# Gram products of the weights after their sign step, in a rebuilt order: sparse attention, a Fourier mixing step and a two-layer network on one core

## The chip, the cores and the metric

The kernel runs on one core of a Trainium2 chip. A core has a matrix engine (TensorE, PE; the profile keeps its weight loads apart as PEld), a vector engine (VectorE, DVE), an activation engine (ScalarE, ACT), a general engine (GpSimd, POOL) and a sync engine (SyncE, SP) whose queue issues nearly all DMAs here. Each engine takes its instructions in the order in which they were issued. The metric is the device time of one execution in microseconds (us).

## The reference

Eight batches of 576 tokens, eight heads of 64. Heads 0 to 3 attend to the last 32 tokens, heads 4 to 7 to tokens a multiple of 32 back. The result x (8 x 576 x 512) goes through the real part of a two-dimensional Fourier transform, a layer norm and a network of width 2048:

```
attn = softmax(mask(q @ k.T / 8)) @ v
x = attn, heads side by side              # 8 x 576 x 512
u = x + real(fft(fft(x, axis=1), axis=2))
un = (u - mean(u)) / sqrt(var(u) + 1e-6)
out = u + relu(un @ w_ch1) @ w_ch2        # 512 -> 2048 -> 512
```

All inputs are float32, but for the two weights, which are numpy float64 by promotion and reach the kernel as 64-bit words.

## The kernel before, in words

**Numbers.** PE multiplies 16-bit numbers fastest, so the kernel splits each operand into a high and a low float16 half and adds three products (high x high, high x low, low x high). Only the first batches' attention and batch 0's transform are done in float32.

**Weights.** W1 (w_ch1) and W2 (w_ch2) come in 16 pieces each, 128 x 512 numbers of 64 bits, loaded by SP into staging tiles. `weights(wi, i)` (L1096) turns piece i into float32 in place of its final tile W. Its steps: c1 on ACT (L1113) scales the upper words; cl on ACT or DVE (L1117, L1119) shifts the lower words; c2 on DVE (L1123) joins both into the magnitude, without the sign; c3 puts in the sign bit, on DVE (L1129) or, as an alternative, on ACT and POOL (L1131 to L1133). Step c5 releases the staging tile, so that the next load that wants it can go.

**Gram products.** `gram_piece` (L1148) multiplies the upper 16 bits of a piece with themselves, 4 products of 128 x 128 on PE (L1158), summed in PSUM. Their diagonal holds sums of squares, for which the sign doesn't matter. From it come, on DVE (L1176 to L1178) and PE (L332), the scales: one per quarter of W1 (`quarter`) and, once all 16 pieces are in, those of W2 (`weights2`). Then `split` (L1197, L1199) and `scaled` (L1232, L1234 and a DMA, L1236) make the float16 halves. The up products (`ups`, L1278) need W1's halves, the down products (`downs`, L1317) W2's.

**Attention and transform.** `att_first` does batch 0's four pairs of heads in float32 from loads of its own (L650 for q and k, L664 for v), in the order ORD0 = 3, 2, 0, 1. `att_pair32` and `att_pair` do the later ones. `fft_batch` builds sums and differences on DVE and POOL (L834), two products on PE (for batch 0 in float32 at L977, L978 and L1003), and the sum u (L1008).

**Chunks.** 18 chunks of 256 tokens: `norm` makes mean and variance (L1060, L1061), the root on POOL (L1066), the normalised token on DVE (L1073), its high half on ACT (L1079), its low half on DVE or POOL (L1082) and a transposing DMA (L1084). Then 8 up products of 24 matmuls, relu twice on ACT (L1293, L1294), the low half of the hidden layer on POOL (L1296), 8 down products of 24 matmuls, and the final sum on DVE (L1325).

**What sets the order.** A planner written in the kernel (`Order`) runs while the program is built. Every step is a generator that yields an `op` with its engine, an estimated duration, buffers to take and give back, and events that it needs and sets. The planner keeps a clock for each engine, picks the earliest step (ties within a window go by a priority, the thread's bias), issues its instructions, and moves on. Where a step has alternatives (`alt`), it takes the engine that would end first by its clock plus a price. When PE would be idle by its clock, `rest` fills the gap with products of zeros into an open Gram accumulator (L1166). All durations, prices and priorities are constants in the table `P`; the true order of the reads and writes is kept by semaphores between the engines. `spawn(gram_piece(...))` in `weights` starts the Gram thread; a thread's first step is planned at the time at which it is spawned.

Of the kernel before, what the change touches and what calls it, by code (L numbers as in the profile page):

```python
# [19 lines left out]
B, H, S, D = 8, 8, 576, 64  # L20

P = dict(
    SL2=1.57, SLD2=2.778, GL0=8, LAT=0.637, GL=6.45, t2=9.759, l0=-28.888, a0=-20, sq0=7.465, w0a=25.925, c=-26.309,
    z=12.736, f0=-22.976, w0=-25.887, s0=-1.061, w1=2.262, s1=-12.582, p0=-14.949, p1=10.996, pn=-3.093, a1=-18.418,
    f1=-1.718, a2=1.463, f2=8.266, an=8.66, fn=-33.229, db=1.762, up=20.1, dn=20.114, ev=0.829, WS=0.0, WV=0.068,
    WA=0.0, WG=0.789, WT=0.095, SL=0.0, SLD=1.95, np=3, AL=3.136, SG=2.918, Lcl=0.553, Lfs=-0.174, Lwl=4.986,
    Lul=-7.793, LO=-11.521, LE=4.84, Lc2=-1.49, LSD=-13.798, Lsub=2.836, Lsub0=20.543, Lrt=20.361, Lu=4.381,
    ORD0=(3, 2, 0, 1), vo=([], [], [], [0, 1, 2, 3]), S0=('qk', 'qk', 'kt', 'pt'),
    S1=('kt', 'pt', 'f6', 'u', 'uT', 'qk', 'f6', 'kt', 'uT', 'u', 'f6', 'kt', 'pt', 'uT', 'u', 'f6'), HB=4, RB=1,
)  # L30
ORD0 = P["ORD0"]
FP32 = {(b, hp) for b in range(3) for hp in range(4)}
# [121 lines left out]
AL, SG = P["AL"], P["SG"]  # L154
# [19 lines left out]
WT = {e: P["W" + e] for e in "SVAGT"}  # L174


class Order:
# [13 lines left out]
    def spawn(self, gen, bias=None, at=None):  # L191
        th = [gen, self.bias if bias is None else bias, self.now if at is None else at, None]
        self.step(th, None)
# [80 lines left out]
def body(ctx: ExitStack, tc: tile.TileContext, a, out):  # L274
# [13 lines left out]
    spawn = S_.spawn  # L288
    SL, SLD = P["SL"], P["SLD"]
# [88 lines left out]
    def att_pair(b, hp):  # L378
# [20 lines left out]
        A.activation(jk[0:vp, 0:vw], vn[0:vp, 0:vw], AF.Square, accum_out=ss[0:vp, 2:3])  # L399
        yield op("T", 0.06, get="big", note=f"total {nm}", slack=P["SL2"])  # L400
        pn = psbig(f"n{nm}")[:, 0:3]
# [694 lines left out]
    def weights(wi, i):  # L1096
# [24 lines left out]
        F = W.rearrange("p a b -> p (a b)").bitcast(F32)  # L1121
        Fi = F.bitcast(I32)
        V.scalar_tensor_tensor(out=Fi, in0=wh, scalar=3, in1=wl, op0=ALU.logical_shift_left, op1=ALU.bitwise_or)  # L1123
        spawn(gram_piece(wi, i, F))

        o = op("V", 0.8, note=f"c3 {wi} {i}", alt=dict(A=(0.67, SG)))
        yield o
# [2 lines left out]
        else:  # L1130
            A.activation(wl.bitcast(F32), wh.bitcast(F32), AF.Sign)  # L1131
            yield op("G", 1.4, note=f"c4 {wi} {i}")
            G.tensor_tensor(out=F, in0=F, in1=wl.bitcast(F32), op=ALU.mult)  # L1133
        yield op(o.engine.replace("A", "G"), 0, put=kind or "", sets=f"sign{wi}_{i}", note=f"c5 {wi} {i}")

    def gram_open(wi, q):

# [311 lines left out]
```

## Time and profile before

| what | value |
|---|---|
| three timed runs | 983.55 us median (978.34 to 986.63) |
| the profiled execution's own time | 983.61 us |
| its span, first to last instruction | 981.8 us |
| mean granted clock of PE | 0.973 |
| busy share PEld, DVE, ACT, POOL | 67%, 59%, 46%, 29% |
| DMA moved | 107.12 MB, 109 GB/s over the span |

The span is the profiled execution from its first to its last instruction. The granted clock is the share of full speed that PE was given. A group in the profile is written as line, engine, operation, out<-in, shapes and count, then busy time and mean duration of one in ns, then the idle time of the engine just before these instructions and what ended it. In the timeline a row has its start, its length, engine, line and operation, and in brackets the idle time before it with the releaser. A row in the list of waits has the waiting engine and line, what it waited for, the total in us, the number of waits and the longest.

### The profile page before, as it was taken

The page shows a single profiled execution, that of the slowest core. Times are in us where ns is not written, and L with a number is a line of the kernel's source. Part 1 is how long each engine was busy: PE and PEld are TensorE (multiplying, and loading weights), DVE is VectorE, ACT ScalarE, POOL GpSimd, SP SyncE. Part 2 cuts the span into 40 slices and gives each one's busy share as a digit, 9 for nine tenths or more (in the row PEclk, how much of TensorE's full clock was granted, in tenths as well). Part 3 has the DMA queues.
Part 4 walks back from the last instruction along what each step waited for, and adds up shares of the span by engine and source line. Part 5 has one row for each costly group of instructions (what it writes and reads, how often), then busy time and mean ns, then how long its engine had stood idle before and what let it go on. Part 6 is the DMA issues. An engine that isn't in the chain of part 4 may idle for free.

```text
span 981.8 us, 23873 instructions
## 1 busy us (share of the span) xinstructions
PE 939.3 (96%) x10017; PEld 659.7 (67%) x10018; DVE 574.7 (59%) x1129; ACT 452.2 (46%) x891; POOL 286.3 (29%) x297
## 2 busy tenths in 40 slices
PE   6779879999999999999999999999999999999998
PEld 6657764676766667676766676667666676676674
DVE  5785896756888588758765957587727221202000
ACT  2744765354565366555745564556423322222121
POOL 0120221223433343334324422442334122222121
PEclk7868998999999999999999999999999999999999
DMA  9757536804533644184537442743240101201000
GB/s 296 240 196 262 170 109 213 187 17 134 133 104 83 150 154 113 35 173 136 123 70 191 97 113 39 225 96 97 59 120 11 34 18 33 32 12 43 1 23 21
DMA packets 135452, 107.12 MB, mean 109 GB/s; under 512 B 103337, under 2 KB 113833, under 8 KB 135345
## 3 DMA queue, kind: packets, MB, share of 16 engines
q1 hardware_dynamic: 132784, 97.22, 37.0%
q0 software_dynamic: 2560, 8.39, 2.8%
q8 instruction: 78, 1.28, 0.6%
q14 instruction: 30, 0.24, 0.1%
HBM read 64.24 MB, written 18.89 MB: 85 GB/s over the span
## 4 chain that ended last, share of the span: by engine, by line
PE 82%; DVE 8%; DMA 5%; ACT 2%; issue 1%; SPq 1%; POOL 0%; ACTq 0%; DVEq 0%; POOLq 0%
PE ph L1278 35%; PE acc L1317 35%; PE B L954 2%; DMA uT<-unp 2%; PE A L931 1%; PE s L456 1%; DMA W<-in_w 1%; DVE W L1123 1%; PE o L487 1%; PE A L978 1%; PE A L977 1%; DMA mloc<-in_mloc 1%; DVE W L1129 1%; PE o L494 1%; DMA q<-in_w 1%
## 5 line engine op out<-in xcount | busy, mean ns | idle before, releaser
L1278 PE MATMUL ph<-uT,W 128*128 128x256 f16 x3456 | 395.4, 273 | 3.3 <-DMA uT<-unp 2.1
L1317 PE MATMUL acc<-W,h 128*128 128x512 f16 x1728 | 390.1, 381 | 2.1 <-POOL ss L393 1.6
L1278 PEld LDWEIGHTS <-W 128*128 128x128 f16 x3456 | 335.2, 98 | 53.8 <-DMA uT<-unp 2.4
L1296 POOL TENSOR_TENSOR h<-hf,h 128x512 f16<-128x512 f32 x144 | 184.5, 1282 | 461.2 <-ACT h L1294 337.8
L1317 PEld LDWEIGHTS <-h 128*128 128x128 f16 x1728 | 166.5, 98 | 191.7 <-issue 5.8
L1293 ACT ACTIVATE hf<-ph 128x512 f32<-128x512 f32 x144 | 85.8, 596 | 299.3 <-PE ph L1278 268.1
L1294 ACT ACTIVATE h<-ph 128x512 f16<-128x512 f32 x144 | 85.3, 592 | 0.0
L1325 DVE SCALAR_TENSOR_TENSOR u<-acc,cout,u 128x512 f32<-128x512 f32 x32 | 23.3, 745 | 101.5 <-PE acc L1317 100.4
L1082 DVE TENSOR_TENSOR unp<-un,unp 128x512 f16<-128x512 f32 x36 | 33.5, 932 | 48.3 <-ACT unp L1079 48.2
L1073 DVE TENSOR_SCALAR un<-u,mv,rstd 128x512 f32<-128x512 f32 x32 | 19.1, 596 | 52.1 <-POOL rstd L1066 50.8
L1066 POOL TENSOR_TENSOR rstd<-mv,negh 128x1 f32<-128x1 f32 x36 | 23.5, 657 | 76.1 <-DVE mv L1063 75.9
L433 DVE SCALAR_TENSOR_TENSOR kt<-qk,sc,kt 128x576 f16<-128x576 f32 (+1 forms) x40 | 36.6, 954 | 12.0 <-ACT kt L418 9.0
L1045 ACT ACTIVATE pq<-B,fcm 128x128 f32<-128x128 f32 (+7 forms) x105 | 27.3, 377 | 16.0 <-PE B L954 8.2
L1166 PE MATMUL gram<-oneb,zero 128*128 128x128 bf16 x427 | 34.0, 246 | 0.0
L468 ACT ACTIVATE sm<-sm 128x594 f32<-128x594 f32 (+1 forms) x20 | 16.3, 816 | 34.8 <-DVE sm L751 34.7
L1166 PEld LDWEIGHTS <-zero 128*128 128x128 bf16 x427 | 30.9, 113 | 2.0 <-issue 1.2
L418 ACT ACTIVATE kt<-qk,sc 128x576 f16<-128x576 f32 (+1 forms) x40 | 29.4, 788 | 3.9 <-DVE sc L374 3.2
L1079 ACT CAST unp<-un 128x512 f16<-128x512 f32 x36 | 22.1, 615 | 16.9 <-DMA uT<-unp 8.8
L1037 DVE TENSOR_TENSOR rt<-pq 128x257 f32<-128x257 f32 (+1 forms) x42 | 17.1, 449 | 21.7 <-ACT pq L1045 19.4
L751 DVE TENSOR_TENSOR sm<-sm,mx 128x594 f32<-128x594 f32 (+1 forms) x32 | 29.4, 919 | 0.3
L749 DVE TENSOR_REDUCE mx<-sm 128x11 f32<-128x594 f32 (+1 forms) x32 | 29.0, 907 | 0.4
L944 DVE SCALAR_TENSOR_TENSOR AT<-A,AT 128x290 f16<-128x290 f32 (+3 forms) x35 | 15.4, 481 | 21.5 <-ACT AT L939 20.5
(202 smaller groups left out, 1044.8 us busy)
## 6 DMA issues: line engine op xcount, KB each, us to landing
qk<-in_qk SPq DMA_DIRECT2D x28, 592.0 KB
sa<-in_w SPq DMA_DIRECT2D x20, 512.0 KB
out<-u SPq DMA_DIRECT2D x32, 256.0 KB
vn<-in_vl SPq DMA_DIRECT2D x10, 432.0 KB
W<-in_w SPq DMA_DIRECT2D x8, 512.0 KB
xd<-xo SPq DMA_DIRECT2D x16, 256.0 KB
xa<-xd SPq DMA_DIRECT2D x8, 512.0 KB
vn<-in_vs SPq DMA_DIRECT2D x10, 384.0 KB
```

What stands on the lines that cost most here:

```text
L418: A.activation(hi, src, AF.Copy, scale=f)
L433: V.scalar_tensor_tensor(out=lo, in0=src, scalar=f, in1=hi, op0=ALU.mult, op1=ALU.subtract)
L749: V.tensor_reduce(out=mx[:, 0:nb], in_=sm, axis=AX.X, op=ALU.max)
L751: on(o).tensor_tensor(out=sm, in0=sm, in1=mx[:, 0:nb].rearrange("p (g o) -> p g o", o=1).to_broadcast([128, nb, w]), op=ALU.subtract)
L1045: A.activation(dst, ps[0:r, c0:c1], AF.Copy, scale=cm[0:r])
L1082: on(o).tensor_tensor(out=unp[:, 1], in0=un, in1=unp[:, 0], op=ALU.subtract)
L1166: T.matmul(idle[-1][:, 0:128], zerb, oneb, start=False, stop=False)
L1278: T.matmul(ph[:, i, :], W1[:, 4 * (f0 // 512) + d, x, f0 % 512 : f0 % 512 + 128], self.uhl[y][:, d, :], start=(n == 0), stop=(n == 11))
L1293: A.activation(hf, ph, AF.Relu, scale=HS)
L1294: A.activation(hh, ph, AF.Relu, scale=HS)
L1296: G.tensor_tensor(out=hl, in0=hf, in1=hh, op=ALU.subtract)
L1317: T.matmul(self.acc[s], (hh, hl)[x][:, i, 128 * s : 128 * s + 128], W2[:, f, 1 - y, :], start=(f == 0 and n == 0), stop=(f == 15 and n == 2))
```

## The change

In `weights`, the line that starts the Gram thread moves from between c2 and c3 to the end, behind c5, so that its products read the piece with its sign; c3 then comes ahead of them in the program. It gets a bias of its own, LG. And the table of the planner's constants is another one, so that the order of all steps is built anew. The constants used below: `Lul`, the price of doing L1082 on DVE (its alternative to POOL); `Lsub`, the price of POOL for the subtraction at L751; `GL`, the planner's time for a gather to land; `vo`, behind which load of q and k each of the first batch's v loads is issued (before, all four behind the last; after, one behind the second, two behind the third, one behind the last); `S0` and `S1`, the kind of staging tile of W1's last four pieces and of W2's pieces.

```diff
 P = dict(
-    SL2=1.57, SLD2=2.778, GL0=8, LAT=0.637, GL=6.45, t2=9.759, l0=-28.888, a0=-20, sq0=7.465, w0a=25.925, c=-26.309,
-    z=12.736, f0=-22.976, w0=-25.887, s0=-1.061, w1=2.262, s1=-12.582, p0=-14.949, p1=10.996, pn=-3.093, a1=-18.418,
-    f1=-1.718, a2=1.463, f2=8.266, an=8.66, fn=-33.229, db=1.762, up=20.1, dn=20.114, ev=0.829, WS=0.0, WV=0.068,
-    WA=0.0, WG=0.789, WT=0.095, SL=0.0, SLD=1.95, np=3, AL=3.136, SG=2.918, Lcl=0.553, Lfs=-0.174, Lwl=4.986,
-    Lul=-7.793, LO=-11.521, LE=4.84, Lc2=-1.49, LSD=-13.798, Lsub=2.836, Lsub0=20.543, Lrt=20.361, Lu=4.381,
-    ORD0=(3, 2, 0, 1), vo=([], [], [], [0, 1, 2, 3]), S0=('qk', 'qk', 'kt', 'pt'),
-    S1=('kt', 'pt', 'f6', 'u', 'uT', 'qk', 'f6', 'kt', 'uT', 'u', 'f6', 'kt', 'pt', 'uT', 'u', 'f6'), HB=4, RB=1,
+    LG=-0.124, SL2=1.538, SLD2=2.133, GL0=8.37, LAT=0.97, GL=20.125, t2=9.759, l0=-30.073, a0=-18.97, sq0=7.465,
+    w0a=18.394, c=-24.962, z=2.858, f0=-26.909, w0=-29.649, s0=0.533, w1=1.247, s1=-16.058, p0=-16.817, p1=10.038,
+    pn=-3.093, a1=-16.706, f1=-1.842, a2=11.395, f2=1.591, an=11.507, fn=-36.503, db=1.762, up=20.1, dn=20.117,
+    ev=0.829, WS=0.0, WV=0.068, WA=0.0, WG=0.732, WT=0.076, SL=0.0, SLD=1.664, np=3, AL=4.076, SG=2.953, Lcl=1.904,
+    Lfs=2.517, Lwl=4.927, Lul=4.132, LO=-16.048, LE=4.469, Lc2=-1.124, LSD=-13.949, Lsub=8.559, Lsub0=20.543,
+    Lrt=20.361, Lu=4.145, ORD0=(3, 2, 0, 1), vo=([], [0], [1, 2], [3]), S0=('qk', 'pt', 'kt', 'qk'),
+    S1=('u', 'pt', 'f6', 'kt', 'u', 'uT', 'f6', 'kt', 'uT', 'u', 'f6', 'kt', 'pt', 'uT', 'qk', 'f6'), HB=4, RB=1,
 )
...
         V.scalar_tensor_tensor(out=Fi, in0=wh, scalar=3, in1=wl, op0=ALU.logical_shift_left, op1=ALU.bitwise_or)
-        spawn(gram_piece(wi, i, F))
 
         o = op("V", 0.8, note=f"c3 {wi} {i}", alt=dict(A=(0.67, SG)))
...
         yield op(o.engine.replace("A", "G"), 0, put=kind or "", sets=f"sign{wi}_{i}", note=f"c5 {wi} {i}")
+        spawn(gram_piece(wi, i, F), bias=P["LG"])
```

## The prediction

> **What bounds the kernel now.** I read the page first, then the busy time by stages, then the list of waits, then the timeline around the Gram products.
>
> ```profile
> span 981.8 us, 23873 instructions
> PE 939.3 (96%) x10017; PEld 659.7 (67%) x10018; DVE 574.7 (59%) x1129; ACT 452.2 (46%) x891; POOL 286.3 (29%) x297
> ...
> L1278 PE MATMUL ph<-uT,W 128*128 128x256 f16 x3456 | 395.4, 273 | 3.3 <-DMA uT<-unp 2.1
> L1317 PE MATMUL acc<-W,h 128*128 128x512 f16 x1728 | 390.1, 381 | 2.1 <-POOL ss L393 1.6
> ...
> L1166 PE MATMUL gram<-oneb,zero 128*128 128x128 bf16 x427 | 34.0, 246 | 0.0
> ```
>
> TensorE (PE) is busy 96% of the span, and 785 of its 939 us are the two big products, which the change leaves alone. But 34.0 us of that busy time is L1166, products with zeros that only fill planned gaps. So about 42 us idle and 34 us of fill are all that another order can win. Where they lie is seen by stages (columns: length, then busy time and instructions of each engine, granted clock, DMA share, GB/s):
>
> ```profile
> 0.00:50.00 50.00, 35.87 (x598) 31.04 (x599) 32.90 (x70) 25.46 (x41) 6.69 (x10) 0.83 0.83 268
> 50.00:64.70 14.70, 9.63 (x129) 8.72 (x126) 14.57 (x22) 2.68 (x8) 4.83 (x4) 0.80 0.73 271
> 64.70:79.80 15.10, 14.77 (x42) 8.55 (x43) 5.77 (x13) 7.33 (x13) 1.19 (x2) 0.50 0.31 106
> 79.80:107.40 27.60, 23.29 (x347) 19.92 (x348) 23.30 (x53) 18.27 (x33) 1.13 (x2) 0.95 0.83 266
> 107.40:133.00 25.60, 23.72 (x233) 20.95 (x231) 20.62 (x32) 15.86 (x28) 12.47 (x7) 1.00 0.35 113
> 133.00:148.90 15.90, 7.89 (x208) 6.66 (x208) 13.76 (x36) 9.75 (x16) 1.71 (x2) 0.96 0.53 151
> ...
> 300.00:500.00 200.00, 200.00 (x2465) 137.61 (x2464) 149.47 (x297) 112.63 (x228) 71.35 (x74) 1.00 0.47 115
> ```
>
> From 300 to 500 us PE has no gap: there no other order of the vector work is worth anything, unless it makes a new gap. Everything is decided in the first 150 us. There three stages matter: 64.7 to 79.8 us (PE busy, but at a clock of 0.50, while VectorE, DVE, is idle for 9 of 15 us), 107.4 to 133 us (the first chunk's up products, nearly dense) and 133 to 148.9 us, where PE is idle for 15.90 - 7.89 = 8.0 us before the first down product.
>
> **What the change does to the weights' steps.** Before, the Gram product of a weight piece is handed out between the step that joins the bits (L1123, "c2") and the step that puts in the sign (L1129, "c3"), and both the product and c3 touch the same tile W. So c3, which overwrites W, must wait until PE has read it. After, c3 stands first and PE waits for it.
>
> ```profile
> DVE W L1129 <- PE gram L1158: 8.1, 1, 8.1
> ...
> PE gram L1158 <- DVE W L1123: 12.2, 12, 3.6
> ```
>
> ```profile
> 71.02 1.28 DVE L1123 SCALAR_TENSOR_TENSOR W<-sa 128x512 int32<-128x512 int32 x2
> ...
> 79.73 1.04 PE L1158 MATMUL gram<-W 128*128 128x128 bf16 x8
> ...
> 80.38 1.29 DVE L1129 SCALAR_TENSOR_TENSOR W<-sa,W 128x512 int32<-128x512 int32 x2 [8.08 <-PE gram L1158]
> ```
>
> The wait of DVE for PE shows once, and it is long: two joins are done at 72.3 us, their Gram products stand in PE's queue behind the spectrum's products until 79.73, and the two sign steps behind them start at 80.38. For 8.08 us everything on DVE stands still: the next pieces, the release of their staging tiles, and so the loads on SP's queue that need those tiles. The queue's own waits over 50 to 110 us show who felt it:
>
> ```profile
> SPq L1108 <- DVE W L1129: 11.7, 7, 4.1
> ...
> SPq L546 <- DVE W L1129: 7.3, 1, 7.3
> ```
>
> Seven weight loads (L1108) and one load of batch 1's q and k (L546) waited for sign steps.
>
> Term 1, **this stall goes.** With c3 ahead of the product, nothing on DVE waits for PE there. 8.1 us hold almost six pairs of c2 and c3 at 0.69 us each (1.29 for two in the rows above). What ends later for it now is the conversion of W2, whose scale needs all 16 pieces, and behind it the first down product:
>
> ```profile
> 129.90 0.69 DVE L1129 SCALAR_TENSOR_TENSOR W<-sa,W 128x512 int32<-128x512 int32 x1
> ...
> 133.88 1.31 PE L1158 MATMUL gram<-W 128*128 128x128 bf16 x20
> ...
> 136.37 0.67 DVE L1176 TENSOR_TENSOR gd<-gram,ident 128x512 f32<-128x512 f32 x1
> ...
> 146.11 2.56 SPq L1236 DMA_DIRECT2D W<-fs  x4
> ...
> 148.20 0.16 PE L332 MATMUL n<-vsum,oneb 128*128 128x1 bf16 x1 [3.91 <-ACT jk L557]
> 148.92 3.57 PE L1317 MATMUL acc<-W,h 128*128 128x512 f16 x8 [0.56 <-DMA W<-fs]
> ```
>
> The last piece is signed at 130.59, the norm starts at 136.37, the first scaled piece leaves at 146.11 and PE starts on it at 148.92. PE was out of up products at 133. If the pieces come up to 8.1 us sooner, the first down product can follow at about 141 to 143. Bounds: nothing (if the loads or ScalarE, ACT, pace the pieces instead) to the whole idle time of that stage, 8.0 us. Some 2 us of those 8.0 belong to attention's own copies and would stay; I take **-6.0 us**.
>
> Term 2, **the clock behind that gap.** The first twelve products of the down block took longer than the next twelve:
>
> ```profile
> 148.92 5.28 PE L1317 MATMUL acc<-W,h 128*128 128x512 f16 x12 [0.56 <-DMA W<-fs]
> ...
> 155.05 2.75 PE L1317 MATMUL acc<-W,h 128*128 128x512 f16 x12
> ```
>
> That is 5.28 - 2.75 = 2.5 us lost right after a wait of 3.91 us. If the gap shrinks below that, the loss goes with it; between 0 and -2.5 I take **-2.5**, since term 1 already assumes that the gap closes.
>
> Term 3, **PE now waits for c3 instead of c2.** PE waited 12 times, 12.2 us in all, for c2; each such wait can grow by one 0.69 us step, 8.3 us at most. In the first 107 us most of that only replaces fill, and at the end of W2 it costs nothing (the last sign step ends 3.3 us before the last Gram products start). Not covered are the products that stand just ahead of the first up product, which starts at 107.4:
>
> ```profile
> 103.72 0.41 PE L1158 MATMUL gram<-W 128*128 128x128 bf16 x4 [1.02 <-DVE W L1123]
> ...
> 106.13 0.40 PE L1158 MATMUL gram<-W 128*128 128x128 bf16 x4 [0.51 <-DVE W L1123]
> ```
>
> Two waits, +1.4 us if both count. I take half, **+0.7** (bounds 0 and +8.3), since the new order counts the sign step in where it places these products. W1's four norms also start one step later, +0.69 us each, hidden behind the spectrum's products (15.1 us) and batch 0's sums.
>
> Term 4, **the rebuilt order.** The constants that choose engines and priorities are new. The one that I can follow to an instruction count is the price of doing the normalised token's low half on DVE: it goes from -7.793 to 4.132, so the planner will mostly hand L1082 to GpSimd (POOL). Groups (busy time, mean ns, idle before and its releaser):
>
> ```profile
> L1296 POOL TENSOR_TENSOR h<-hf,h 128x512 f16<-128x512 f32 x144 | 184.5, 1282 | 461.2 <-ACT h L1294 337.8
> ...
> L1082 DVE TENSOR_TENSOR unp<-un,unp 128x512 f16<-128x512 f32 x36 | 33.5, 932 | 48.3 <-ACT unp L1079 48.2
> ```
>
> L1296 is the same subtraction on POOL: 1.28 us in place of 0.93, so up to 36 x 1.28 = 46 us more on an engine that is busy 29%, and 33.5 us plus 48.2 us of waits less on DVE. In the dense stretch neither is on the path; before the first up product two of them stand in its chain, +0.35 us each, **+0.7**. The second is the first batch's loads: three v loads now go ahead of the last q and k.
>
> ```profile
> v<-in_v SPq DMA_DIRECT2D x1, 438.8 KB
> ...
> v<-in_v SPq DMA_DIRECT2D x1, 390.0 KB
> ```
>
> Two of 390 KB (the other goes to another tile of that size) and one of 438.8 KB are 1219 KB, at the first stage's 268 GB/s some 4.6 us later for the last pair's scores. Its cover:
>
> ```profile
> 19.86 1.05 DVE L751 TENSOR_TENSOR sm<-sm,mx 128x864 f32<-128x864 f32 x1
> ...
> 27.09 0.92 ACT L688 ACTIVATE sm<-sm 128x864 f32<-128x864 f32 x1
> ```
>
> The last pair's scores were ready for ACT at 20.9 and taken at 27.1, 6.2 us later; so **0** (and +4.6 if ACT now comes earlier). Other staging tiles for W2's pieces are the same kinds in another order: 0, part of term 1's doubt. For all other priorities no row gives a price. Their bound is what the start holds: half of the half-clock stage (15.1 / 2 = 7.5 us) to the good, and as much to the bad; I take **0**.
>
> Sum, against the profiled execution's own time of 983.61 (span 981.8; the three timed runs have the median 983.55, so the same sum holds for it): 983.6 - 6.0 - 2.5 + 0.7 + 0.7 = **976.5 us**, 0.7% less. A run of this kernel is told from no change at about 1%, so this forecast itself lies within that.
>
> [...] Ahead of the half-clock stage stands PE's longest wait for c2:
>
> ```profile
> 58.07 0.41 PE L1158 MATMUL gram<-W 128*128 128x128 bf16 x4 [3.56 <-DVE W L1123]
> ```
>
> After it the granted clock is 0.50 from 64.7 to 79.8 us, though PE is busy 14.77 of 15.10 us. [...]
>
> **Rivals.**
>
> (a) The start runs warm (0.27). If the new order closes the 3.56 us gap at 54.5 to 58, the fp32 products of 64.7 to 79.8 run at full clock and everything behind them starts up to 15.1 / 2 = 7.5 us sooner: 976.5 - 7.5 = 969 us. For it: the gap is one wait for a c2 that stood behind batch 0's sums on DVE. Against: after the change the same product waits for c3 too.
>
> (b) The gap only moves (0.17). W2's pieces are paced by their loads and by ACT, 15.9 of 25.6 us busy from 107.4 to 133, not by DVE; the first down product stays at about 149 us: 983.5 us. For it: in 133 to 148.9 the wait named longest is PE's for ACT's squares (3.91 us), not for W2. Against: the first down product waited for its weights even behind that wait (0.56 us).
>
> (c) The low halves on POOL make PE wait, slower (0.17). POOL takes its instructions in order. A low half that waits for ACT's cast holds up the hidden layer's L1296 behind it; that holds the single fp32 tile hf, so the next relu, so the PSUM tile of the next up product.
>
> ```profile
> DVE unp L1082 <- ACT unp L1079: 48.2, 20, 5.9
> ...
> L1296 POOL TENSOR_TENSOR h<-hf,h x144: 1147/1157/4482, 111.6 to 968.8; 128x512 f16<-128x512 f32 x144
> ...
> 324.73 5.18 PE acc L1317 x24
> ```
>
> DVE waited 20 times for that cast, 2.4 us each, 5.9 at the longest. The cover is a pair of down products, 5.18 us in the chain: 2.4 + 1.16 + 1.16 (two POOL steps, at the median) = 4.7 us still fits; from a wait of 2.9 us on it doesn't. At 4.15 us, midway between mean and longest, 20 waits cost 1.3 us each, 25 us in all: 1001 us. Against: a planner that knows POOL's queue can place the low half behind the cast.
>
> That the sign step isn't moved for all pieces is no rival: all 32 pieces run the same lines.
>
> **How the numbers follow.** Forecast 0.39, (a) 0.27, (b) 0.17, (c) 0.17. The range of the forecast alone is 970 to 983. For eight in ten I go down to 963 (case (a) with the rest of the fill at the start cut too) and up to 992, which leaves out most of (c). Faster by over 1% means under 973.7: nearly all of (a) and a third of the forecast, 0.39. Slower by over 1% means over 993.4: most of (c) and a small rest of (b), 0.15. Within 1%: 0.46.
>
> **What would show it.** Right: no wait of L1129 for L1158, and PE's waits at L1158 now name L1129; the first product of L1317 at 140 to 144 us in place of 148.9 and at 2.75 us per twelve; fill (L1166) at or under 34 us; PE idle between 107 and 149 us under 4 us in place of 9.9. Low halves of unp under POOL, about 30 of 36, and PE still without gaps from 300 to 500 us. Wrong: the first down product at 148 us or later (then term 1 failed); PE waits for h, hf or uT in the dense stretch (then (c)); a granted clock near 1 in the spectrum's first products (then (a)).

## The result and the profile after

The changed kernel takes **992.24 us** (median of four runs, 990.33 to 994.42), the kernel before on the same chip 981.5 (978.34 to 986.63): 1.0115 times as long, with a 95% interval of 1.007 to 1.0159. On a second chip the ratio was 1.0107 (1.0076 to 1.0138). The change makes the kernel about 1.1% slower; 976.5 was predicted. A ratio below compares the undisturbed runs of two kernels on one chip, while a median is that of all runs; where runs spread widely, the two can differ by some tenths of a per cent.

The page of the changed kernel, in the rows that answer to those shown of before (its profiled execution took 991.3 us, its mean granted clock was 0.966 against 0.973):

```profile
span 989.5 us, 23813 instructions
...
PE 940.7 (95%) x10012; PEld 665.2 (67%) x10013; DVE 556.3 (56%) x1090; ACT 454.4 (46%) x894; POOL 328.8 (33%) x335
...
L1278 PE MATMUL ph<-uT,W 128*128 128x256 f16 x3456 | 395.1, 274 | 3.8 <-DMA uT<-unp 3.8
L1317 PE MATMUL acc<-W,h 128*128 128x512 f16 x1728 | 391.1, 381 | 0.4 <-DVE u L1325 0.4
...
L1082 POOL TENSOR_TENSOR unp<-un,unp 128x512 f16<-128x512 f32 x36 | 42.5, 1180 | 48.5 <-ACT unp L1079 41.0
...
L1166 PE MATMUL gram<-oneb,zero 128*128 128x128 bf16 x422 | 38.0, 262 | 0.2 <-issue 0.2
```

PE's work is the same, the span 7.7 us longer. All 36 low halves went to POOL, VectorE (DVE) lost 18 us of work, fill rose from 34.0 to 38.0 us. Where the 7.7 us lie is seen by stages. Before (length, busy time and count of PE, PEld, DVE, ACT, POOL, then granted clock, DMA share, GB/s):

```profile
0.00:50.00 50.00, 35.87 (x598) 31.04 (x599) 32.90 (x70) 25.46 (x41) 6.69 (x10) 0.83 0.83 268
50.00:100.00 50.00, 42.59 (x419) 32.90 (x417) 36.24 (x74) 21.52 (x43) 7.15 (x7) 0.76 0.65 222
100.00:150.00 50.00, 37.78 (x533) 32.30 (x534) 42.81 (x82) 33.40 (x58) 14.18 (x9) 0.98 0.48 147
150.00:200.00 50.00, 47.89 (x473) 29.98 (x472) 37.48 (x67) 22.71 (x42) 11.95 (x12) 0.92 0.72 192
200.00:250.00 50.00, 48.42 (x496) 34.97 (x495) 28.48 (x66) 24.09 (x55) 15.82 (x24) 1.00 0.33 92
250.00:300.00 50.00, 49.75 (x572) 35.19 (x570) 38.77 (x72) 30.69 (x66) 16.93 (x19) 1.00 0.43 106
```

The changed kernel:

```profile
0.00:50.00 50.00, 32.73 (x570) 29.58 (x571) 29.22 (x59) 23.67 (x38) 5.59 (x8) 0.84 0.86 256
50.00:100.00 50.00, 42.41 (x434) 34.25 (x432) 38.35 (x79) 24.13 (x48) 16.68 (x14) 0.79 0.66 227
100.00:150.00 50.00, 40.37 (x538) 36.03 (x537) 42.90 (x81) 33.47 (x59) 15.44 (x13) 0.86 0.56 152
150.00:200.00 50.00, 47.09 (x508) 30.54 (x508) 31.57 (x50) 23.15 (x39) 8.77 (x8) 0.93 0.56 169
200.00:250.00 50.00, 42.71 (x453) 28.75 (x452) 35.32 (x85) 21.06 (x50) 20.12 (x28) 0.92 0.44 122
250.00:300.00 50.00, 49.86 (x584) 35.85 (x582) 37.55 (x66) 32.46 (x64) 19.53 (x19) 0.98 0.42 97
300.00:500.00 200.00, 199.99 (x2322) 138.61 (x2321) 137.49 (x274) 108.18 (x219) 81.84 (x82) 1.00 0.47 117
```

Three stages are worse. From 0 to 50 us PE is idle 17.3 us in place of 14.1. From 200 to 250 us it is idle for 50 - 42.71 = 7.3 us in place of 1.6, and its clock is 0.92 in place of 1.00. From 100 to 150 us, the stage that the prediction was about, PE is idle 9.6 us in place of 12.2, but at a clock of 0.86 in place of 0.98; the first up product comes at 110.77 (107.42 before). From 300 to 500 us PE is as dense as before.

What happens at 200 to 250 us is the start of chunk 2's up products. Waits and timeline of PE there:

```profile
PE ph L1278 <- DMA uT<-unp: 3.8, 1, 3.8
PE s L456 <- ACT kt L418: 2.8, 1, 2.8
PE s L456 <- DVE kt L433: 0.7, 1, 0.7
```

```profile
237.99 0.17 PE L332 MATMUL n<-ss,oneb 128*128 128x3 bf16 x1
240.97 0.22 PE L456 MATMUL s<-kt 64*64 64x54 f16 x4 [2.81 <-ACT kt L418]
241.89 0.97 PE L456 MATMUL s<-kt 64*64 64x54 f16 x62 [0.70 <-DVE kt L433]
246.64 10.80 PE L1278 MATMUL ph<-uT,W 128*128 128x256 f16 x72 [3.78 <-DMA uT<-unp]
```

Before, the same up products began without a wait, behind a dense queue:

```profile
236.67 0.93 PE L534 MATMUL o<-vsx,pT 54*64 54x65 f32 x48
237.53 5.41 PE L1278 MATMUL ph<-uT,W 128*128 128x256 f16 x48
```

PE waits 7.3 us in three pieces, and then 72 products take 10.80 us where 48 took 5.41, so 72 would take 8.1: 2.7 us more for the half clock behind the waits. The longest wait leads back to VectorE, whose order puts batch 1's tail sums (L1037, L1008) ahead of the second normalised tile (L1073):

```profile
234.25 0.74 DVE L1037 TENSOR_TENSOR rt<-pq 33x257 f32<-33x257 f32 x2
...
236.51 0.55 DVE L1073 TENSOR_SCALAR un<-u,mv,rstd 128x512 f32<-128x512 f32 x1
```

Before, that tile came first and the tail sums later:

```profile
226.49 0.55 DVE L1073 TENSOR_SCALAR un<-u,mv,rstd 128x512 f32<-128x512 f32 x1
...
232.02 0.74 DVE L1037 TENSOR_TENSOR rt<-pq 33x257 f32<-33x257 f32 x2
```

In the changed kernel the tile's transposing DMA is issued at 240.43 only, and what it brings lands just ahead of 246.64.

### The profile page after: what moved, and what is told of

Read it like the earlier page. It is cut to its first block, busy times and chain, and to the rows that moved or that the text cites. A ratio compares the mean times of both kernels' runs of the same rounds, so it can differ in the third digit from the quotient of the medians.

```text
span 989.5 us, 23813 instructions
## 1 busy us (share of the span) xinstructions
PE 940.7 (95%) x10012; PEld 665.2 (67%) x10013; DVE 556.3 (56%) x1090; ACT 454.4 (46%) x894; POOL 328.8 (33%) x335
## 4 chain that ended last, share of the span: by engine, by line
PE 86%; DMA 7%; DVE 3%; POOL 1%; SPq 1%; ACT 1%; issue 1%; DVEq 0%; ACTq 0%; POOLq 0%
PE ph L1278 38%; PE acc L1317 36%; DMA W<-in_w 2%; PE B L954 2%; DMA vsx<-in_v 2%; PE A L931 1%; PE s L456 1%; PE o L487 1%; PE gram L1166 1%; PE o L494 1%; DMA qk<-in_qk 1%; PE s L515 1%; DMA uT<-unp 1%; POOL xb L824 1%; PE A L978 1%
## 5 line engine op out<-in xcount | busy, mean ns | idle before, releaser
L1296 POOL TENSOR_TENSOR h<-hf,h 128x512 f16<-128x512 f32 x144 | 180.9, 1257 | 429.7 <-ACT h L1294 339.7
L1082 POOL TENSOR_TENSOR unp<-un,unp 128x512 f16<-128x512 f32 x36 | 42.5, 1180 | 48.5 <-ACT unp L1079 41.0
L1073 DVE TENSOR_SCALAR un<-u,mv,rstd 128x512 f32<-128x512 f32 x32 | 18.1, 565 | 51.3 <-POOL rstd L1066 41.6
L433 DVE SCALAR_TENSOR_TENSOR kt<-qk,sc,kt 128x576 f16<-128x576 f32 (+1 forms) x40 | 37.6, 979 | 12.1 <-ACT kt L418 11.2
L1166 PE MATMUL gram<-oneb,zero 128*128 128x128 bf16 x422 | 38.0, 262 | 0.2 <-issue 0.2
L1166 PEld LDWEIGHTS <-zero 128*128 128x128 bf16 x422 | 34.3, 122 | 5.1 <-issue 4.5
L1066 POOL TENSOR_TENSOR rstd<-mv,negh 128x1 f32<-128x1 f32 x36 | 23.4, 656 | 41.4 <-DVE mv L1063 37.7
L1045 ACT ACTIVATE pq<-B,fcm 128x128 f32<-128x128 f32 (+7 forms) x105 | 27.3, 382 | 17.5 <-PE B L954 10.7
L751 DVE TENSOR_TENSOR sm<-sm,mx 128x594 f32<-128x594 f32 (+1 forms) x32 | 31.5, 985 | 0.5
L824 POOL DMA_INDIRECT xb<-xd,ridx x24 | 29.1, 1214 | 7.3 <-issue 5.8
L1037 DVE TENSOR_TENSOR rt<-pq 128x257 f32<-128x257 f32 (+1 forms) x42 | 15.9, 419 | 22.0 <-POOL h L1296 20.5
```

The lines of the kernel that those rows point to most:

```text
L433: V.scalar_tensor_tensor(out=lo, in0=src, scalar=f, in1=hi, op0=ALU.mult, op1=ALU.subtract)
L751: on(o).tensor_tensor(out=sm, in0=sm, in1=mx[:, 0:nb].rearrange("p (g o) -> p g o", o=1).to_broadcast([128, nb, w]), op=ALU.subtract)
L824: gathers[b] = G.indirect_dma_start(out=dst, out_offset=None, in_=xd[b], in_offset=bass.IndirectOffsetOnAxis(ap=ridx[:, n : n + 1], axis=0),)
L1082: on(o).tensor_tensor(out=unp[:, 1], in0=un, in1=unp[:, 0], op=ALU.subtract)
L1166: T.matmul(idle[-1][:, 0:128], zerb, oneb, start=False, stop=False)
L1296: G.tensor_tensor(out=hl, in0=hf, in1=hh, op=ALU.subtract)
```

## Experiments

The theory with which I began: the change as planned is harmless, and chunk 2's late supply is the loss. The rivals: the Gram behind the sign step costs by itself; the loss is spread over the start; the half clock is the loss; any other order costs. The numbers of a run are its median, and the ratio to the kernel before on the same chip with its interval. Waits and starts are those of its profiled execution.

**Each half alone.** Before's table with only the Gram thread moved behind c5 (bias -0.124, as in the new table):

```diff
-        spawn(gram_piece(wi, i, F))
...
+        spawn(gram_piece(wi, i, F), bias=-0.124)
```

> The table of constants of before, with the Gram thread started after the sign step as in the changed kernel. Theory T (the rebuilt table costs the time): no wait of the sign step for PE any more, and 978 to 985 us, within 0.5% of before. Theory G (the later Gram products cost it, because PE now waits for one more step of every piece): 989 to 994 us, as the changed kernel.

987.29 us, 1.0106 (1.0071 to 1.0141). And the new table with the Gram thread where it was:

```diff
+        spawn(gram_piece(wi, i, F), bias=P["LG"])
...
-        spawn(gram_piece(wi, i, F), bias=P["LG"])
```

> The changed kernel's table, with the Gram thread started ahead of the sign step as before. Theory T: 988 to 994 us, as the changed kernel. Theory G: 978 to 985 us, as before.

991.73 us, 1.0156 (1.011 to 1.0202). Either half alone costs as much as both, so they don't add, and neither theory is borne out alone. Both runs share one thing with the changed kernel: the planner built a new order. They lose at different places. With the Gram alone, PE's first up product comes at 113.72 and the first down product at 159.35, and at 237 us there is no wait; with the table alone the first down product comes at 143.43, the earliest of all, and between 237 and 247 us PE waits 2.8 us for the squares and 6.3 for kt.

**The stall alone, with the order all but held.** W1's magnitudes are built in the staging tile, the Gram reads them there, and c3 writes the final tile, so it has nothing to wait for. The staging tile is then released by the Gram product and no longer by c5. The order of PE and POOL is that of before, and so is VectorE's but for one small fill instruction; two loads of W2's pieces stand some places later on SP's queue, and these pieces' scaling steps (L1113, L1117) some places later on ACT's:

```diff
-        V.scalar_tensor_tensor(out=Fi, in0=wh, scalar=3, in1=wl, op0=ALU.logical_shift_left, op1=ALU.bitwise_or)
-        spawn(gram_piece(wi, i, F))
+        own = wi == 0; X = wl if own else Fi; V.scalar_tensor_tensor(out=X, in0=wh, scalar=3, in1=wl, ...)
+        spawn(gram_piece(wi, i, stg.bitcast(BF16)... if own else F.bitcast(BF16)..., kind or "" if own else ""))
...
-            V.scalar_tensor_tensor(out=Fi, in0=wh, scalar=-(2**31), in1=Fi, op0=ALU.bitwise_and, op1=ALU.bitwise_or)
+            V.scalar_tensor_tensor(out=Fi, in0=wh, scalar=-(2**31), in1=X, op0=ALU.bitwise_and, op1=ALU.bitwise_or)
...
-        yield op(o.engine.replace("A", "G"), 0, put=kind or "", ...)
+        yield op(o.engine.replace("A", "G"), 0, put="" if own else kind, ...)
...
-        yield op("T", 0.24, ..., sets=f"gram{wi}_{i}", ...)
+        yield op("T", 0.24, ..., sets=f"gram{wi}_{i}", put=free, ...)
```

> The kernel before with its order kept on all engines (two weight loads of the sync queue excepted, which stand some places later): W1's bits are put together in the staging tile, the Gram reads them there, and the sign step writes the weights' place, so that it need not wait for the Gram. It removes the 8.08 us stall of VectorE without moving the Gram and without a new order. Theory of the prediction's first term (the stall sets when the first down product starts): first down product 4 to 7 us earlier than 148.92, 971 to 975 us, 0.993 to 0.996 of the kernel before. Rival (the stall is filled again by loads and by the order of VectorE's queue, so it was worth nothing): first down within 1.5 us of 148.9, 0.998 to 1.002.

978.8 us, 1.0016 (0.9997 to 1.0036). The stall is gone, and the run is no shorter. VectorE's waits in this run and the instruction that now waits:

```profile
DVE u L1008 <- PE B L1004: 11.7, 2, 10.1
```

```profile
73.11 1.29 DVE L1129 SCALAR_TENSOR_TENSOR W<-sa 128x512 int32<-128x512 int32 x2
84.48 0.76 DVE L1008 TENSOR_TENSOR u<-B,xa 128x257 f32<-128x257 f32 x2 [10.09 <-PE B L1004]
```

Next in VectorE's queue stand batch 0's sums, which need the spectrum's products B. Before, they waited 1.94 us behind the stall; now they wait 10.09. 8.08 + 1.94 = 10.02: the stall has moved on by a few instructions, whole. The first down product came at 147.21 (148.92 before), again behind a 3.96 us wait for ScalarE's squares; 1.5 us of the difference were there at the first up product already (105.96 in place of 107.42). This run doesn't test the loads, though: with the staging tiles released by the Gram, the two loads of W2 that were issued at 72.95 and 73.35 before come at 80.96 and 84.98. The next run tests both.

**The Gram behind the sign step, with the order held.** Here c3 is issued right ahead of the piece's Gram products if it hasn't been yet, which is the change's first half without a new plan. PE's, ACT's, POOL's and SP's instructions stand in the order of before, and on VectorE only sign steps stand earlier:

```diff
+        signed = []; sign = lambda: signed or signed.append(V.scalar_tensor_tensor(out=Fi, in0=wh, ...) or 1)
-        spawn(gram_piece(wi, i, F))
+        spawn(gram_piece(wi, i, F, sign))
...
-        if o.engine == "V":
-            V.scalar_tensor_tensor(out=Fi, in0=wh, ...)
+        if o.engine == "V" or signed:
+            sign()
...
-        Fb = F.bitcast(BF16).rearrange("p (n t) -> p n t", t=2)[:, :, 1]
+        sign(); Fb = F.bitcast(BF16).rearrange("p (n t) -> p n t", t=2)[:, :, 1]
```

> The kernel before with the planner's order kept, and the sign step of a piece issued at the latest right ahead of its Gram products, which then read the signed numbers. The order on TensorE, ScalarE, GpSimd and the sync queue is word for word that of before; on VectorE only the sign steps stand some places earlier. This is the first half of the change without the second. Theory (the rebuilt order is what costs): 0.997 to 1.003 of the kernel before, the stall of 8.08 us gone. Rival (TensorE's wait for one more step costs, the prediction's third term and more): 1.004 to 1.011, as in the run that moved the Gram and built a new order.

1.0017 (0.9984 to 1.0051); the median of its twelve runs is 982.88 against 977.36, but they spread from 974.82 to 990.84, so this run excludes a cost of half a per cent less firmly than its interval says. It does exclude a gain of the size predicted. VectorE's wait for B is 7.2 us in all (3.3 before): about half of the 8.08 us went there, and the rest of the stall is shorter because the spectrum's first products, which VectorE waits for, took 9.8 us in this execution and 15.0 in that of before, where half clock covered all of them.

The first down product came at 144.85, 4.1 us sooner than before, but not because the gap ahead of it closed. 1.9 us of the 4.1 were there at the first up product (105.50 in place of 107.42), and 3.7 at the end of chunk 0's last one (129.36 in place of 133.05). From there to the first down product it takes 15.5 us, where before took 15.9, with the same wait for the squares and the same half clock behind it:

```profile
144.26 0.16 PE L332 MATMUL n<-vsum,oneb 128*128 128x1 bf16 x1 [3.87 <-ACT jk L557]
144.85 5.28 PE L1317 MATMUL acc<-W,h 128*128 128x512 f16 x12 [0.42 <-DMA W<-fs]
```

PE's price for waiting for one more step (the last row ends with the view):

```profile
101.24 0.40 PE L1158 MATMUL gram<-W 128*128 128x128 bf16 x4 [2.22 <-DVE W L1124]
101.84 0.41 PE L1158 MATMUL gram<-W 128*128 128x128 bf16 x4 [0.20 <-DVE W L1124]
...
105.50 0.73 PE L1278 MATMUL ph<-uT,W 128*128 128x256 f16 x3
```

2.22 + 0.20 = 2.4 us ahead of the first up product, where before had four waits, 1.02 + 0.20 + 0.51 + 0.20 = 1.9. Behind the longer wait PE ran at half clock for 3.4 us, from 102.6 on, so that from the end of the fill ahead of these waits to the first up product it took 6.5 us (99.02 to 105.50) in place of 4.7 (102.71 to 107.42).

**One constant, and a new order.** If a new order costs by itself, a single constant must do it. Two were taken from the new table and put into the kernel before; the Gram stays where it was:

```diff
-    ... GL=6.45, ...
+    ... GL=20.125, ...
```

> The kernel before with one constant of its table changed to the changed kernel's: the time after which a gather of batch 1 to 7 is counted as landed, 20.125 in place of 6.45, and its whole order built anew from it. Theory (each table of constants is fitted to its own graph, and any other order costs): 1.006 to 1.016 of the kernel before, with low-clock stretches between 100 and 300 us that the kernel before lacks. Rival (the constants that do harm are those of the start): 0.998 to 1.004.

998.29 us, 1.0222 (1.0189 to 1.0255). `GL` is only the planner's belief about a gather; the gather itself is the same, and each engine has as many instructions as before (10,017 on PE, 1129 on VectorE, 891 on ACT, 297 on POOL). PE's timeline:

```profile
231.93 0.78 PE L456 MATMUL s<-kt 64*64 64x54 f16 x62 [1.81 <-DVE kt L433]
237.17 0.18 PE L332 MATMUL n<-ss,oneb 128*128 128x3 bf16 x1 [4.46 <-ACT jk L399]
242.65 4.60 PE L1278 MATMUL ph<-uT,W 128*128 128x256 f16 x24 [5.29 <-DMA uT<-unp]
```

The changed kernel's loss at chunk 2 is here, with none of its Gram change and one of its constants. Another wait of 6.34 us for a transposed tile came at 856 us. The second constant hands the low halves to POOL:

```diff
-    Lul=-7.793, ...
+    Lul=4.132, ...
```

> The kernel before with one constant of the new table, the price of the normalised tokens' low halves on VectorE (4.132 for -7.793), and its order built anew from it. Theory (any rebuilt order costs at the start and at chunk 2): 1.004 to 1.016. Rival (that constant does nothing): 0.998 to 1.003.

993.15 us, 1.0165 (1.0121 to 1.0209). Here more than the order changes, since all 36 low halves move to POOL. Its losses are other ones; among PE's waits from 100 to 300 us stand two for the hidden layer:

```profile
PE ph L1278 <- ACT h L1294: 2.5, 1, 2.5
PE acc L1317 <- POOL h L1296: 2.5, 1, 2.5
```

They look like the prediction's rival (c), but no low half stands ahead of them on POOL. Ahead of the first, L1296 itself took 5.96 us (110.41 to 116.37); ahead of the second, POOL had waited 5.06 us with the root L1066 for VectorE's mean and variance, and L1082 comes behind L1296, at 245.60.

**The changed kernel with one thing put back.** Three runs undid one constant each in the changed kernel: `GL` to 6.45, the v loads behind the last q, `Lul` to -7.793.

```diff
-    ... GL=20.125, ...
+    ... GL=6.45, ...
```

> The changed kernel with one constant set back: the planner's time for a gather to land, 20.125 to 6.45. The program is the same up to about 170 us. Theory T with the gather as its largest part: batch 1's first sum (L834) at 180 to 186 us in place of 194.8, its transform's first product at about 201 in place of 208.9, the waits of PE at 238 to 247 us (2.8 + 0.7 + 3.8 us and a cold clock after them, 10.8 us for 72 products in place of 7.9) gone: 981 to 986 us. If the gather is not it: 989 to 994 us.

994.64 us, 1.0188 (1.0135 to 1.0241): missed. Batch 1 came early as wanted, and chunk 2's transposed tile was still 5.2 us late.

```diff
-    ... vo=([], [0], [1, 2], [3]), ...
+    ... vo=([], [], [], [0, 1, 2, 3]), ...
```

> The changed kernel with the first batch's v loads all behind the last q and k, as before. If the first loads are a part of the loss: the last pair's scores at 13 to 14 us in place of 19.3, batch 0's first sum at 53 to 55 us in place of 59.0, and 985 to 989 us. If that is absorbed later, as the prediction had it: 989 to 994 us.

988.59 us, 1.014 (1.009 to 1.019): the first up product came at 106.06 (110.77 in the changed kernel), and the lead was gone at 245 us, with waits of 4.0 us for kt and 5.3 for uT.

```diff
-    ... Lul=4.132, ...
+    ... Lul=-7.793, ...
```

> The changed kernel with one constant put back: the low halves of the normalised tiles (L1082) may go to VectorE early again, as before. Theory (the time is lost at 220 to 260 us, where chunk 2's transposed tiles come late): POOL's low half of the last tile of chunk 2 ends at most 1 us sooner on VectorE, so the loss at 220 to 260 stays and the run is at 988 to 993 us. Rival of the prediction (low halves on POOL make TensorE wait): the time falls to 975 to 983 us.

993.12 us, 1.0165 (1.0119 to 1.0212), as the theory of chunk 2 said; its wait for uT there is 10.6 us. The same constant costs 1.7% when it is put into the kernel before and gains nothing when it is taken out of the changed one. So it isn't the constant that is good or bad.

**Mending chunk 2.** The changed kernel, with batch 1's tail sums behind both normalised tiles of chunk 2 (the plan has that rule for batch 0 already):

```diff
-        yield op(... need="un0_0 un0_1" if t == 2 and b == 0 else "", ...)
+        yield op(... need=f"un{2 * b}_0 un{2 * b}_1" if t == 2 and b < 2 else "", ...)
```

> The changed kernel with one dependency added in the plan: batch 1's tail sums wait until both tiles of chunk 2 are normalised, as batch 0's already do for chunk 0. Theory: TensorE's wait for chunk 2's transposed tile (3.78 us at 243 to 247) shrinks to under 1 us and its first up product starts at 240 to 243 instead of 246.64; TensorE's waits for the float16 tile kt (3.51) stay; 986 to 989 us. Rival (the loss is spread, or sits in the start): no change, 990 to 994 us.

991.33 us, 1.0144 (1.0096 to 1.0192). Missed: its wait for uT is 4.05 us, not under 1. The tile came earlier (first up product at 241.22), but the new order had PE there earlier too. With the scores of batch 3's pair 2 put behind the first up products:

```diff
-        yield op(... get="big", put="kt", note=f"scores {nm}", ...)
+        yield op(... get="big", put="kt", need="first2" if nm == f"3_{ORD0[1]}" else "", note=f"scores {nm}", ...)
...
-                yield op(... sets=f"up{c}" if fp == 7 else "", ...)
+                yield op(... sets=f"up{c}" if fp == 7 else "first2" if (c, fp) == (2, 0) else "", ...)
```

> The changed kernel with another dependency added: the scores of batch 3's pair 2, which stand ahead of chunk 2's first up products in TensorE's queue, come behind them. Theory: the transposed tile still lands near 246.6, so the waits for kt only turn into a longer wait for it (7 to 12 us in place of 3.78), the first up starts at 245 to 247; 990 to 993 us. Rival (the queue order alone is the fault): first up at 240 or sooner, 984 to 987 us.

998.58 us, 1.0204 (1.016 to 1.0247). The wait went where the theory said, into one longer one:

```profile
247.60 7.54 PE L1278 MATMUL ph<-uT,W 128*128 128x256 f16 x48 [8.47 <-DMA uT<-unp]
```

The time rose all the same, with one more wait at 683 us, 4.6 us for a transposed tile of attention (L494). Both together:

> Both added dependencies together. Theory: chunk 2's first up starts at 236 to 241, TensorE waits under 3 us between 225 and 250 us, and the run is at 980 to 986 us. Rival (loss spread over the kernel, or given back later): the stretch of 225 to 250 us is repaired but the time stays at 989 to 994 us.

1011.49 us, 1.0335 (1.0296 to 1.0373), the slowest of all: PE waits 6.44 us for squares and 4.29 for uT at 242 to 253 us, and again 3.64, 4.01, 3.63 and 2.19 us at 446 to 463. And the first rule together with the v loads put back:

> The changed kernel with two edits: all loads of v behind the last q as before, and batch 1's tail sums behind the normalised tiles of chunk 2. Theory (both losses are real and add): first up product at 104 to 107 us, no wait over 2 us for chunk 2's transposed tile, 978 to 984 us, 1.000 to 1.006 of the kernel before. Rival (an early start is given back later whatever is mended): 988 to 993 us, 1.010 to 1.016.

990.43 us, 1.0147 (1.011 to 1.0185); the first up product came at 107.68, and PE waits 2.8 us for kt, 3.0 for the squares and 4.6 for uT. My first theory falls with these four: chunk 2's supply is where the changed kernel loses, but as a symptom. Each rule that mends it builds another order, which loses there or elsewhere.

**The changed kernel once more.**

> The changed kernel unchanged, on this chip: 1.010 to 1.016 of the kernel before. Theory (chunk 2's supply is lost in each execution, the start varies): TensorE's waits at 238 to 247 us come again within 0.5 us each, while the low-clock stretch over the float32 products differs from the 6.8 and 10.2 us at 65 to 85 us. Rival (the profiled execution was an unusual one): the waits at 238 to 247 us are not there.

989.09 us, 1.0107 (1.0076 to 1.0138). The same three waits came again:

```profile
PE ph L1278 <- DMA uT<-unp: 3.1, 1, 3.1
PE s L456 <- ACT kt L418: 2.8, 1, 2.8
PE s L456 <- DVE kt L433: 0.7, 1, 0.7
```

So the place of the loss belongs to the order and not to one execution; the wait for uT came as 3.1 us in place of 3.8, a little more apart than the 0.5 that I had allowed. The start does vary: the low clock over the float32 products lasted 27.3 us from 70.0 on, where the first execution had 6.8 and 10.2, while batch 0's E began at 53.05 and not at 59.01. Both executions come to the first up product within a microsecond (111.59 and 110.77).

**Is it the clock?** The sum of 50 us x (1 - granted clock) over the stages shown up to 300 us is 25.5 us before and 34.0 after, 8.5 more for 7.7 us of span. To keep the clock up I put products with zeros into PE's queue ahead of the waits; the order is otherwise held:

```diff
+    ... warm = lambda o, n: [T.matmul(o, zerb, zero.to_broadcast([128, 512]), start=True, stop=True) for _ in range(n)]
...
+    ... warm(ps[:, 0:512], 12 if (b, hp) == (3, 2) else 0)
...
+    ... warm(ph, 16 if (c, fp) == (2, 0) else 0) ...
```

> As the run with four fills, but with the two at chunk 2 alone (12 ahead of the scores, 16 ahead of the first up product). Theory: the 10.2 us at half clock from 242 us are gone (200 to 250 us at 1.00 in place of 0.92) and 72 up products take 7.9 us in place of 10.80; 3 to 5 us less than the changed kernel, 1.006 to 1.010 of the kernel before. Rival: no change, 1.010 to 1.016.

994.77 us, 1.0158 (1.0126 to 1.019). The clock there was 1.00, and the time did not fall:

```profile
245.18 0.30 PE L456 MATMUL s<-kt 64*64 64x54 f16 x8 [0.50 <-issue]
245.41 3.67 PE L334 MATMUL ph<-zero 128*128 128x512 bf16 x16
248.92 8.02 PE L1278 MATMUL ph<-uT,W 128*128 128x256 f16 x72
```

The 72 products now take 8.02 us, but they start at 248.92, behind the fill, and end at 256.94 where they ended at 257.44. With fill ahead of two more waits (the totals at 102 and 151 us):

> The changed kernel with zero products put into TensorE's queue ahead of four of its waits, and nothing else: 8 ahead of the total at 102 us, 16 ahead of the total at 151 us, 12 ahead of batch 3's scores at 241 us, 16 ahead of chunk 2's first up product at 247 us. The waits stay as long as they are; only TensorE is not idle in them. Theory (the loss is the clock: half speed for 6.8 us from 102, 13.7 from 143 and 10.2 from 242 us): the granted clock stays at or near 1.00 there, which gives back 10 to 15 us of the 15.4 that half speed costs, and the run is at 0.997 to 1.003 of the kernel before. Rival (the waits themselves are the loss, and the clock only follows): 1.010 to 1.016, as the changed kernel.

997.68 us, 1.0183 (1.015 to 1.0215). And in the kernel before, at its own two waits:

```diff
+    ... warm(pv[:, 0:512], {(1, 1): 16}.get((b, hp), 0)) ...
...
+    ... warm(ph, 8 if (c, fp) == (1, 0) else 0) ...
```

> The kernel before with zero products ahead of two of its waits: 16 ahead of the total at 148 us, 8 ahead of chunk 1's first up product at 181 us. Theory: the 6.8 us at half clock from 147.5 and the 3.4 from 181.7 are gone; 3 to 5 us less than before, 0.995 to 0.997. Rival (the fills run into the work behind them, or the clock falls all the same): 1.000 to 1.004.

981.2 us, 1.0015 (0.9993 to 1.0037). The clock was 1.00 from 100 to 300 us, the first twelve down products took 2.75 us in place of 5.28, and the runs are no shorter. The fill was sized too long in places (at chunk 2 it ran past the landing of the tile, and in the run with four fills 16 of them took 6.38 us at half clock), so these three don't settle what the half clock is worth by itself. They do show that fills of these sizes are no repair.

## Why the prediction was wrong

**Term 1, the stall (-6.0): the step that failed is "the first down product can follow".** That L1129's wait for L1158 would go was right; that something behind it would come sooner was not. In the run with the Gram on the staging tile the same 8.08 us came back, as part of a wait of ten, at the next instruction of VectorE that needs PE, because both waits end with the same thing: PE getting through the spectrum's products of batch 0. I had followed the stall's followers (loads, staging tiles, W2) and not VectorE's own next instruction. The row was there to read: batch 0's sums stood four steps behind the stalled ones, with 1.94 us of wait left.

Nor did the pieces set the time of W2's scale. The prediction's rows show that too: the last Gram products of W2 start at 133.88, without a wait, behind chunk 0's last up product in PE's queue and 3.3 us after the last sign step. 12.2 us later the first scaled piece leaves (146.11). With the Gram on the staging tile these were 132.41 and 144.54, 12.1 us apart, and in the held run 130.19 and 142.18, 12.0 us apart, each time just behind the last up product. So pieces that are signed sooner don't bring the first down product closer to the up products while PE's queue has these Gram products there. In the changed kernel it has them there too (134.97); the last piece of W2 was signed at 132.08 (130.59 before), and the first down product came at 151.15, not at 141 to 143. Worth: nothing that these runs can tell from no change, 1.0016 and 1.0017.

**Term 2, the clock behind the gap (-2.5): failed with term 1.** The wait ahead of the first down product, for ScalarE's squares, did not depend on W2. In the changed kernel:

```profile
151.12 0.16 PE L332 MATMUL n<-vsum,oneb 128*128 128x1 bf16 x1 [3.76 <-ACT jk L557]
151.15 5.28 PE L1317 MATMUL acc<-W,h 128*128 128x512 f16 x12
```

3.76 us for 3.91, and the same 5.28 us for twelve products. The prediction gave this row as evidence for rival (b). (b) was right that the gap stays, 17.0 us from the last up to the first down product in place of 15.9, but not that loads and ACT pace the pieces: PE's queue does, as said above.

**Term 3, PE waits for c3 (+0.7): right in kind, and near in size.** The prediction counted two waits ahead of the first up product and left out two of 0.20 us. With the order held they grew from 1.9 to 2.4 us, +0.5; with the half clock behind them that stretch grew by 1.8 us. In the held run the wait of 2.22 us was followed by 3.4 us at half clock, and in the changed kernel one of 2.07 us ahead of 102.14 by 6.8. In all, PE's waits for these steps grew from 12.2 to 15.2 us. And in the changed kernel the planner gave two of the 32 sign steps to ACT and POOL (L1132), which the prediction left out of account; PE waited 2.2 and 5.2 us for them in the two executions.

**Term 4, the rebuilt order (0): the term that decided, and mis-sized.** I gave it no price and bounds of 7.5 us either way, drawn from the start alone, since "everything is decided in the first 150 us". The changed kernel loses at 200 to 250 us, past that. Of the 14.8 us between 976.5 and the profiled execution's 991.3, terms 1 and 2 make 8.5; the other 6.3 fall to the rebuilt order and to what term 3 had too small, and lie within the bounds. A new order by itself costs 2.2% in the run that changed `GL` alone, and 1.65% in the one that changed `Lul`, where the low halves move as well; the changed kernel's 1.1% is below both. Twelve different rebuilt orders ran here, and all twelve are slower than before, by 1.1 to 3.4%. Nine of them, the changed kernel's among them, share the new table; that it is not the table's fault alone is shown by the other three, which have before's table but for one constant or for the Gram's place (1.0106, 1.0165, 1.0222). The three kernels that kept before's order, wholly or but for a few steps, lie at 1.0015 to 1.0017.

Of the smaller parts: the low halves were priced at +0.7 for two in the start's chain. All 36 went to POOL, and between 300 and 500 us PE has no gap, so rival (c) did not come in the changed kernel; putting them back gains nothing. No run here shows its mechanism: with that constant alone in the kernel before, PE's two waits of 2.5 us for the hidden layer had other causes than a low half. The v loads ahead of the last q were priced at 0, under the cover of ACT's backlog. Batch 0's last scores did come later, at 18.70 and 19.26 us in the two executions in place of 13.46, and in one of them batch 0's E began at 53.05, as before (53.12): the cover held. In the other, E came at 59.01 behind a slow gather (below). Rival (a), a warm start, came in part: the spectrum's first products took 12.2 us in that execution and 10.8 in the other, in place of 15.0. In the second the half clock then lasted through the rest of the spectrum, to 97 us, and the first up product came no sooner.

Of the signs listed: the waits of L1129 gone, right; first down product at 140 to 144 and at 2.75 us per twelve, wrong (151.15 and 5.28); PE idle under 4 us from 107 to 149, wrong (5.0); fill at or under 34, wrong (38.0, and 34.9 in the second execution); low halves under POOL and PE dense from 300 to 500 us, right.

**What stays open.** That a new order costs is shown; why before's order is better than every other one tried is not. One explanation is that its table was fitted to just this graph of steps, with the planner's durations being only estimates; no run here tests how it came about. If that is so, any new order would lose, whatever edit it came from. Nor is it shown why the run with the tail sums moved, whose profiled execution took 985.38 us, has a median of 991.33.

## What to carry to other kernels

When a kernel's order comes from a planner, an edit of the graph or of one constant is two changes: what it does, and a new order. Hold the order to price the first, and change one harmless constant to price the second, before crediting either; here the first was worth nothing that could be measured, and the second cost 1 to 2%. And before a stall is counted as a gain, read the next instruction on the stalled engine and ask what it waits for: if it is the same engine's later work, the stall only moves.

## What the runs showed of the hardware

**Time goes with the granted clock.** Over the timed runs of both kernels, time x mean granted clock has nearly the same median: 958 for 76 runs of the kernel before (952 to 965) and 957 for ten of the changed one (956 to 960), while their median times are 978 and 990 us. Two of them: 976.74 x 0.981 = 958 before, 991.3 x 0.966 = 958 after. So what makes the changed kernel longer shows as half clock, which doesn't say which of the two is the cause; in the run that changed `GL` alone the product is higher, 969 at the median. In the traces of the kernel before and of the changed one the clock records know only 0.5 and 1.0, and the low stretches, but for the one that the program's end cuts off, last 3.4, 6.8, 13.7 or 23.9 us in the kernel before and 6.8, 10.2 or 13.7 in the changed one (10.2 us from 242.1), whole multiples of 3.4 us. The fills did not turn the clock into a lever: they raised it and not the speed, though some were too long to settle the matter.

**Float32 products took longer than 16-bit ones.** In the kernel before, at a clock of 1.00 (84 to 88 us), ten float32 products of the spectrum, of at most 128 columns (L1003), took 1.39 us from 84.45 to the start of the next product, 0.14 us each, and four 16-bit ones of the Gram, of 128 columns (L1158), 0.23 us from 85.95, 0.06 each.

**POOL can stand still beside VectorE's joins and sign steps.** The hidden layer's L1296 takes 1.16 us at the median. In the kernel before one that began at 111.64 took 4.48 us beside joins and sign steps that VectorE ran back to back to 115.11; in the held run these are 109.77, 2.66 us and 111.41, and in the run with `Lul` changed in the kernel before 110.41, 5.96 us and 115.36. Each of the three ended 1.01 or 1.02 us behind the last of these steps, whenever it had begun. The first costs PE a wait of 1.17 us for h, the last one of 2.5. In the changed kernel one of batch 0's gathers was hit:

```profile
48.18 5.12 POOL L824 DMA_INDIRECT xb<-xd,ridx  x1 [0.30 <-issue]
```

The median of the 24 is 0.96 us. From 48.78 to 52.47 VectorE ran six joins and sign steps; the second execution of the changed kernel agrees, with six steps to 48.14 and a gather of 3.97 us, and in both the gather ends 0.83 us behind the sixth step. The kernel before had 1.35 at the longest. Not each gather beside such steps is slow: one in the kernel before took 0.96 us beside a join and a sign step (44.62).
